# One kernel for memory attention and two MLPs: the first half's instructions keep the order in which the program issues them

## The chip, the core and the metric

The kernel runs on one core of one Trainium2 chip. The metric is the device time of one execution in microseconds (us). Three executions of the kernel before gave 904.52, 904.96 and 908.23 us; their median is 904.96 us.

## What is computed

Three layers run one after the other on B = 4 batches of S = 576 positions (2304 tokens in all). Inputs and weights of the attention are float32; the weights of the two MLPs arrive as float64 and are read as pairs of 32-bit words.

```
a    = softmax over s of phi                      # [b, h, s, 32]
k_m  = einsum('bhsm,bhsd->bhmd', a, k);  v_m the same with v
attn = softmax(q @ k_m^T / 8) @ v_m               # 8 heads of 64
x    = attn as [2304, 512];  xn = x / rms(x) * rms_g
y    = (silu(xn @ w_gate) * (xn @ w_val)) @ w_out     # 512 -> 1536 -> 512
h    = y @ w_in;   g = h if h >= 1, 0 if h <= -1, else (h + 1)^2 / 4
out  = g @ w_out2                                  # 512 -> 2048 -> 512
```

## The kernel before, in words

The program has two halves. **P1** does the attention, the gated MLP and all the turning of weights; its result x2 goes to DRAM as a high and a low part (`x2h_d`, `x2l_d`). **P2** is the second MLP: a plain loop over 5 blocks of tokens and 16 pieces of the inner dimension (`p2_in`, L1034, and `p2_out`, L1059). Every large product is three matmuls (high x high, high x low, low x high).

P1 is a set of Python generators ("streams") that an `Agenda` runs against a model of time. A stream yields what its next step needs: an engine and a duration ("V", 0.69 is 0.69 us of VectorE; P is TensorE, A ScalarE, G GpSimd, D a transfer), a buffer to take or give back, or a flag that another stream sets. The Agenda picks again and again the step that can start first by its model, the lower priority number first among equals, and lets that stream emit its instructions. So the program's order is a schedule worked out by a model of time. The streams are:

- `loads` (L350 on): phi, k, v and q of batch 0, 1, 2, 3 by SP's queue, with model times 1.8 us (phi), 3.6 us each (k, v), 3.4 us (q), 0.45 us each (the four parts of the rest of q), and 1.415 us more until a load has arrived (`DMA_LAG`). The order is phi, k and v, q of batch 0, the same of batch 1, then phi, k and v of batch 2, the rest of q, q of batch 2, and phi, k and v, q of batch 3.
- `soft(b)`: the maximum, difference (L446) and exponential (L453) of phi, then the sums on GpSimd (L460 to L463). Its model times up to the exponential are V 2.12, P 0.25, V 0.29, V 0.42, P 0.3, V 1.35. `memory(b)`: k_m and v_m (kvps, L495) in PSUM banks 7 and 4, then their scaling and `vT`, `vbd`, `kmT`.
- `pair(n)`, nine of them: scores (L621), softmax (L631 to L655), transposes, product with v_m (xp, L684), the norm (L675, L696 to L700), and the split into `Ah`, `Al` (L717, L719).
- `chunk(fc)`, 12 of them, and `convert`: a 512 KB transfer into one of 4 `raw` buffers (L245, model time 1.46), then the float64 words become float32: exponent part on VectorE or ScalarE (L261 or L259), low word on GpSimd or ScalarE (L266 or L264), merged on VectorE (L270), and the sign set on VectorE (L274); the last two have a model time of 0.69 each. A chunk of w_gate and w_val fills a `w` buffer (3 of them, and 2 more in the place of `w2s`) and is stored to DRAM (L325) for the later batches. `wo1_unit` does the same for w_out and `w2_piece` for the second MLP, with a split into high and low (L283, L285).
- `vw`: v_m times a chunk (L763, in PSUM banks 6 and 7), after which the `w` buffer is free; its split is L781, L783. `gv`: the gate and value products (L812, six matmuls each for a half of the positions), and `gate`: L837, L840, L843, L845. `out1`: L870, three matmuls for each of 12 chunks (one step of 0.395, after a flag of that chunk's gate), and x2's split and store (L884 to L894).
- `heat`: small matmuls (L474) that only keep TensorE busy in the beginning.

What the program emits is then ordered anew: a scheduler of the language, with a timing simulation of its own, sorts the instructions of every engine by when it thinks that they are ready. `keep_in_program_order` pins an instruction behind the one that was emitted before it on the same engine; the kernel before uses it for the loads of phi, k, v, q, for the first 24 raw transfers and for the heat matmuls, and for nothing else. Three lines carry the model of what follows what:

```python
HOP = {"P": 0.14, "V": 0.16, "A": 0.16, "G": 0.16, "D": 1.2, "PP": 0.0, "VV": 0.12, "AA": 0.12, "GG": 0.1}
self.free = {"D": 1.7}
starts = [max(at + HOP.get(x[5] + e, HOP[e]), self.free.get(e, 0.0)) for e in kind[: len(times)]]
```

`x[5]` is the engine of the stream's last step: a step on the same engine costs the smaller hop ("PP": 0.0). Passing a flag empties `x[5]`, so that the next step pays the hop of an engine that has to be told by another.

Of the kernel before, what the change touches and what calls it, by code (L numbers as in the profile page):

```python
# [25 lines left out]
ORDER = [0, 1, 2, 3, 8, 4, 5, 6, 7]  # L26

BANKS = {"g": (0, 1), "v": (2, 3), "o": (4, 5), "p": (0, 1, 2, 3), "w": (6, 7), "q": (2, 3), "s": (1,), "x": (2, 3), "a": (0,), "t": (5,), "k": (7,), "m": (4,), "l": (4,)}

KEEP = 24  # L30

HEAT = (6, ("A", (0, 0)), 2.09, 0.34)

# [11 lines left out]
class Agenda:  # L45
# [59 lines left out]
    def run(self, stop=None):  # L105
        while self.live and not (stop and stop in self.flags):
            best = None
            for x in self.live:
                s = self._start(x)
                if s is not None:  # L110
                    key = (max(s[0], self.now), x[0], x[1])
                    if best is None or key < best[0]:
                        best = key, x, s[1]
            assert best is not None, [(x[0], x[3]) for x in self.live]
            (at, _, _), x, z = best
            self.live.remove(x)
            self.now = at
            kind, arg = x[3]
            value = None
            done = at  # L120
            if kind == "take":
                self.room[arg] -= 1
            elif kind == "give":
                self.room[arg] += 1
            elif kind == "rest":
                done += arg
            elif kind == "flag":
                x[5] = ""
            elif kind == "heat":
                tick = int(at / TICK)  # L130
                value = self.ticks.get(tick, 0.0) < HEAT[2]
                if value:
                    slow = 1.0 if self.ticks.get(tick - 1, 0.0) > WARM else 2.0
                    self.ticks[tick] = self.ticks.get(tick, 0.0) + arg
                    done = self.free["P"] = at + arg * slow
            else:
                value = kind[z]
                t = arg[z] if isinstance(arg, tuple) else arg
                if value == "P":
                    tick = int(at / TICK)  # L140
                    slow = 1.0 if self.ticks.get(tick - 1, 0.0) > WARM else 2.0
                    self.ticks[tick] = self.ticks.get(tick, 0.0) + t * DUTY.get(kind, 1.0)
                    t *= slow
                done = self.free[value] = at + t
                x[5] = value
            self.done = done
            x[4] = x[4] + 0.5 if kind == "Dq" else done
            self._go(x, value)


def tile_attn_moe(tc, q, k, v, phi, w_gate, w_val, w_out1, rms_g, w_in2, w_out2, out):
# [10 lines left out]
    nc = tc.nc  # L162
    B, H, S, D = q.shape
    M = phi.shape[3]
# [72 lines left out]
    def convert(src, pieces, dst, split, done):  # L237

        yield "take", "raw"
        yield "D", 1.46  # L240
        n = nconv[0]
        nconv[0] += 1
        raw = wv.tile([P, CU, 2], U32, tag="raw", name=f"raw{n}", bufs=BUFS["raw"])
        rs = raw.rearrange("p n t -> p (n t)")
        i = nc.sync.dma_start(out=rs.rearrange("p (c f) -> p c f", c=pieces) if pieces > 1 else rs, in_=src)  # L245
        if n < KEEP:
            tc.keep_in_program_order(i)
        yield "rest", DMA_LAG
        if split:
            yield "take", "x"  # L250
            x = wv.tile([P, CU], F32, tag="x", name=f"cx{n}", bufs=BUFS["x"])
            dst = x
        hv, low = raw[:, :, 1].bitcast(F32), raw[:, :, 0]
        if len(dst.shape) > 2:
            hv, low = (t.rearrange("p (c f) -> p c f", c=dst.shape[1]) for t in (hv, low))
        du = dst.bitcast(U32)
        eng = yield "VAhi", (0.45, 0.68)
        if eng == "A":
            nc.scalar.activation(out=dst, in_=hv, func=AF.Copy, scale=SHRINK)  # L259
        else:  # L260
            nc.vector.tensor_scalar(out=dst, in0=hv, scalar1=SHRINK, scalar2=None, op0=ALU.mult)  # L261
        eng = yield "GAlow", (0.73, 0.68)
        if eng == "A":
            nc.scalar.activation(out=low, in_=low, func=AF.Copy, scale=LOW_SCALE, bias=LOW_BIAS)  # L264
        else:
            nc.gpsimd.tensor_scalar(  # L266
                out=low, in0=low, scalar1=LOW_SCALE, scalar2=LOW_BIAS, op0=ALU.mult, op1=ALU.add
            )
        yield "V", 0.69
        nc.vector.scalar_tensor_tensor(  # L270
            out=du, in0=du, scalar=3, in1=low, op0=ALU.logical_shift_left, op1=ALU.bitwise_or
        )
        yield "V", 0.69
        nc.vector.scalar_tensor_tensor(  # L274
            out=du, in0=hv.bitcast(U32), scalar=0x80000000, in1=du, op0=ALU.bitwise_and, op1=ALU.bitwise_or
        )
        yield "give", "raw"
        if split:
            hi, lo = split
            if len(hi.shape) > 2:  # L280
                x = x.rearrange("p (c f) -> p c f", c=hi.shape[1])
            yield "A", 0.63
            nc.scalar.activation(out=hi, in_=x, func=AF.Copy)  # L283
            eng = yield "VGlo", (0.69, 1.35)
            (nc.vector if eng == "V" else nc.gpsimd).tensor_tensor(  # L285
                out=lo, in0=x, in1=hi.bitcast(F32), op=ALU.subtract
            )
            yield "give", "x"
        done()
# [60 lines left out]
    def loads():  # L350

        seq = []
        for b in range(B):
            seq += [("phi", b), ("kv", b)]
        for i, pr in zip(Q_AT, q_loads, strict=True):
            seq.insert(i, ("q", pr))
        for s in seq:
            yield "take", "qr" if s[0] == "q" and s[1][0] == B else s[0]
            if s[0] == "phi":
                b = s[1]  # L360
                yield "Dq", 1.8
                t = phi_t[b] = ld.tile([P, 4, J, M], F32, tag="phi", name=f"phi{b}", bufs=BUFS["phi"])
                tc.keep_in_program_order(
                    nc.sync.dma_start(out=t.rearrange("p c j m -> p c (j m)"), in_=by_half(phi[b], J * M))
                )
            elif s[0] == "kv":
                b = s[1]
                t = kv_t[b] = ld.tile([P, 2, 4, J, D], F32, tag="kv", name=f"kv{b}", bufs=BUFS["kv"])
                for i, src in ((0, k), (1, v)):
                    yield "Dq", 3.6  # L370
                    tc.keep_in_program_order(
                        nc.sync.dma_start(
                            out=t[:, i].rearrange("p c j d -> p c (j d)"), in_=by_half(src[b], J * D)
                        )
                    )
            else:
                b = s[1][0]
                yield "Dq", 3.4 if b < B else 0.45 * len(per_batch(s[1]))
                if b == B:
                    t = q_t[s[1]] = ld.tile([P, H, LJ, D], F32, tag="qr", name=f"qr{s[1][1]}", bufs=BUFS["qr"])  # L380
                    for bb, rows in per_batch(s[1]):
                        tc.keep_in_program_order(
                            nc.sync.dma_start(
                                out=t[rows],
                                in_=q[bb, :, SM:S, :].rearrange("h (p j) d -> p h j d", j=LJ),
                            )
                        )
                else:
                    t = q_t[s[1]] = ld.tile([P, H, QJ, D], F32, tag="q", name=f"q{b}", bufs=BUFS["q"])
                    tc.keep_in_program_order(  # L390
                        nc.sync.dma_start(
                            out=t.rearrange("p h j d -> p h (j d)"),
                            in_=q[b, :, 0:SM, :].rearrange("h (p j) d -> p h (j d)", j=QJ),
                        )
                    )
            add(0, arrived(s))
        for name in ("phi", "kv", "q", "qr"):
            for _ in range(BUFS[name]):
                yield "take", name
        mark("inputs")  # L400
# [66 lines left out]
    def heat():  # L467
# [3 lines left out]
        while HEAT[1] not in agenda.flags:  # L471
            go = yield "heat", 0.1067
            if go:
                i = nc.tensor.matmul(  # L474
                    out=t[:, 0:256], lhsT=zeros[:, 0:P], rhs=zeros, start=True, stop=True,
                    skip_group_check=True,
                )
                tc.keep_in_program_order(i)
        yield "give", ("bank", HEAT[0])

    s1_t = {}
# [452 lines left out]
            mark("w2 done")  # L934


    add(0, loads())
    for b in range(B):
        add(P_SOFT + 2 * b, soft(b))
# [76 lines left out]
    for i in range(N2U, N2U + N2R):  # L1016
        load_w2(2 * i + 1, w2c)
    agenda.run()
    left.close()


# [114 lines left out]
```

## Time and profile before

| | us |
|---|---|
| median of three executions | 904.96 |
| the profiled execution, its own time | 907.72 |
| its span | 905.9 |
| TensorE busy in the span | 853.7 |
| VectorE busy | 468.6 |
| ScalarE busy | 333.6 |
| GpSimd busy | 106.4 |
| first matmul of P2 (L1034) | 493.6 |

The span is what the profiler saw of the program, and 1.8 us of the execution lie around it. Matmuls are pipelined, so TensorE's busy time covers overlapping work. The interesting part is P1, from 0 to 493.6 us; after it TensorE runs the two products of P2 one after the other to the end.

### The profile page before, as it was taken

To read this page: it belongs to the slowest core of one execution; us is meant where nothing else is said; L and a number is where in the kernel's file an instruction comes from. 1 tells how busy PE (TensorE), PEld (TensorE's weight loads), DVE (VectorE), ACT (ScalarE), POOL (GpSimd) and SP (SyncE) were. 2 spreads that over 40 slices of the span, in tenths; PEclk is the share of its full clock that TensorE was granted. 3 is DMA by queue.
4 is the path that set the end of the run, shared out by engine and by line. 5 is a ranking of instruction groups with operands and counts; after the bars stand their busy time and mean duration, and the time that the engine had idled before them with its cause. 6 is when DMAs were issued, how large, how long until landed. Compare 5 with 4: busy or idle time off the path is not lost.

```text
span 905.9 us, 15047 instructions
## 1 busy us (share of the span) xinstructions
PE 853.7 (94%) x6058; PEld 732.8 (81%) x6058; DVE 468.6 (52%) x836; ACT 333.6 (37%) x656; POOL 106.4 (12%) x160
## 2 busy tenths in 40 slices
PE   7767889979999999999999999999999999999992
PEld 6655678859988998899999888888888888888892
DVE  3566857987898685405521433433343333333441
ACT  2335556645577355304421222222222222222330
POOL 3135314510000020000020500000000000000000
PEclk9886979969999999999999999999999999999997
DMA  9987233769999998222383980000040003000100
GB/s 321 329 281 244 95 117 111 263 228 330 346 338 342 358 317 291 103 79 94 120 253 111 387 260 1 25 22 1 1 140 0 1 1 93 0 1 1 47 1 24
DMA packets 72142, 137.56 MB, mean 152 GB/s; under 512 B 8840, under 2 KB 37512, under 8 KB 72072
## 3 DMA queue, kind: packets, MB, share of 16 engines
q1 hardware_dynamic: 61576, 108.28, 34.8%
q0 software_dynamic: 10496, 28.32, 10.0%
q8 instruction: 47, 0.77, 0.3%
q14 instruction: 23, 0.19, 0.1%
HBM read 99.35 MB, written 37.22 MB: 151 GB/s over the span
## 4 chain that ended last, share of the span: by engine, by line
PE 83%; DMA 7%; DVE 5%; ACT 2%; issue 1%; POOL 1%; SPq 0%; DVEq 0%; ACTq 0%
PE acc L1059 22%; PE hp L1034 22%; PE ops L870 16%; PE gps L812 7%; PE vps L812 7%; PE vwps L763 3%; DMA raw<-in_moe_w_gate_dram 2%; PE xp L684 2%; DMA phi<-in_phi_dram 1%; DMA raw<-in_moe_w_out_dram 1%; DMA raw<-in_moe_w_val_dram 1%; DVE w L270 1%; DVE w L274 1%; PE heat L474 1%; DMA raw<-in_moe_w_in_dram 1%
## 5 line engine op out<-in xcount | busy, mean ns | idle before, releaser
L1034 PE MATMUL hp<-xh,w 128*128 128x512 f32 (+1 forms) x640 | 193.1, 368 | 0.0
L1059 PE MATMUL acc<-w,gh 128*128 128x512 f32 x576 | 178.4, 391 | 0.0
L1034 PEld LDWEIGHTS hp<-xh,w 128*128 128x128 f32 x640 | 117.0, 188 | 21.5
L1040 DVE SCALAR_TENSOR_TENSOR y<-y 128x512 f32<-128x512 f32 (+1 forms) x80 | 51.1, 639 | 152.0 <-ACT y L1039 152.0
L1059 PEld LDWEIGHTS acc<-w,gh 128*128 128x128 f32 x576 | 107.0, 188 | 22.4
L1034 PE MATMUL hp<-xl,w 128*128 128x512 f32 (+1 forms) x320 | 118.3, 370 | 0.0
L870 PE MATMUL ops<-ah,wo1h 128*128 128x288 f32 x384 | 113.2, 297 | 2.1 <-ACT ah L843 2.1
L870 PE MATMUL ops<-al,wo1h 128*128 128x288 f32 x384 | 113.6, 297 | 1.3 <-DVE al L845 0.7
L870 PE MATMUL ops<-ah,wo1l 128*128 128x288 f32 x384 | 112.9, 295 | 0.1
L1059 PE MATMUL acc<-w,gl 128*128 128x512 f32 x288 | 112.6, 392 | 0.0
L1039 ACT ACTIVATE y<-hp,consts 128x512 f32<-128x512 f32 (+1 forms) x80 | 51.6, 645 | 151.7 <-PE hp L1034 151.7
L1044 ACT ACTIVATE gh<-y 128x512 fp32r<-128x512 f32 (+1 forms) x80 | 47.1, 589 | 137.5 <-PE acc L1059 118.5
L1045 DVE TENSOR_TENSOR gl<-y,gh 128x512 fp32r<-128x512 f32 (+1 forms) x80 | 51.1, 639 | 79.9 <-ACT gh L1044 79.9
L870 PEld LDWEIGHTS ops<-ah,wo1h 128*128 128x128 f32 x384 | 71.9, 188 | 4.2 <-ACT ah L843 2.6
L870 PEld LDWEIGHTS ops<-al,wo1h 128*128 128x128 f32 x384 | 72.3, 188 | 3.2 <-POOL al L845 1.5
L870 PEld LDWEIGHTS ops<-ah,wo1l 128*128 128x128 f32 x384 | 72.2, 188 | 0.3 <-DVE wo1l L285 0.3
L1034 PEld LDWEIGHTS hp<-xl,w 128*128 128x128 f32 x320 | 60.2, 188 | 10.8
L1059 PEld LDWEIGHTS acc<-w,gl 128*128 128x128 f32 x288 | 54.0, 188 | 12.3
L812 PE MATMUL gps<-Ah,vwh 128*128 128x288 f32 x192 | 60.7, 316 | 2.0 <-ACT vwh L781 2.0
L843 ACT ACTIVATE ah<-th 128x288 fp32r<-128x288 f32 x96 | 42.0, 442 | 47.7 <-DVE th L840 47.4
L812 PE MATMUL vps<-Ah,vwh 128*128 128x288 f32 x192 | 58.4, 304 | 0.0
L840 DVE TENSOR_TENSOR th<-th,vps 128x288 f32<-128x288 f32 x96 | 42.9, 449 | 29.4 <-PE vps L812 29.4
(116 smaller groups left out, 1366.0 us busy)
## 6 DMA issues: line engine op xcount, KB each, us to landing
w<-wf_d SPq DMA_DIRECT2D x36, 512.0 KB, 4.4
w<-w_d POOLq DMA_DIRECT2D x36, 512.0 KB, 8.1
w_d<-w2s SPq DMA_DIRECT2D x32, 512.0 KB, 6.2
raw<-in_moe_w_out_dram SPq DMA_DIRECT2D x28, 512.0 KB, 5.5
raw<-in_moe_w_in_dram SPq DMA_DIRECT2D x16, 512.0 KB, 5.6
raw<-in_moe_w_gate_dram SPq DMA_DIRECT2D x12, 512.0 KB, 6.7
raw<-in_moe_w_val_dram SPq DMA_DIRECT2D x12, 512.0 KB, 6.1
wf_d<-w SPq DMA_DIRECT2D x12, 512.0 KB, 4.4
```

Of the source, the lines that this page charges most:

```text
L684: nc.tensor.matmul(out=xp[rows, 256 * g : 256 * g + 256], lhsT=aT[:, i, g, rows], rhs=vbd_t[bb][:, g].rearrange("p h d -> p (h d)"), start ...
L763: nc.tensor.matmul(out=vps[g][0][32 * c : 32 * c + 32, 2 * P * x : 2 * P * x + 2 * P], lhsT=vT[b][hs, c, :], rhs=t[hs, c].rearrange("p i f ...
L812: nc.tensor.matmul(out=p[:, 0:HB], lhsT=wt[:, g, i, :], rhs=at[b][:, g, c], start=(g == 0 and x == 0), stop=(g == 1 and x == 2),)
L840: nc.vector.tensor_tensor(out=th, in0=th, in1=ps[1][0], op=ALU.mult)
L843: nc.scalar.activation(out=ah, in_=th, func=AF.Copy)
L870: nc.tensor.matmul(out=p[:, 0:HB], lhsT=wt[:, fc, d], rhs=at[:, c], start=(fc == 0 and x == 0), stop=(fc == NF1 - 1 and x == 2),)
L1034: nc.tensor.matmul(out=hp, lhsT=wt[:, kc, :], rhs=xt[:, kc, 0:n], start=(kc == 0 and x == 0), stop=(kc == KC - 1 and x == 2),)
L1039: nc.scalar.activation(out=y, in_=hp, func=AF.Relu, scale=0.5, bias=half)
L1040: nc.vector.scalar_tensor_tensor(out=y, in0=y, scalar=1.0, in1=y, op0=ALU.min, op1=ALU.mult)
L1044: nc.scalar.activation(out=gh, in_=y, func=AF.Copy)
L1045: nc.vector.tensor_tensor(out=gl, in0=y, in1=gh.bitcast(F32), op=ALU.subtract)
L1059: nc.tensor.matmul(out=acc, lhsT=gt[:, cs], rhs=wt, start=(fc == 0 and x == 0), stop=(fc == NF2 - 1 and x == 2),)
```

## The change

The whole of P1 is emitted inside a context in which each engine, and each queue of transfers, issues its instructions in the order in which the program emitted them; P2 stays as it was. The pins are dropped, as that context holds every instruction. In the Agenda, a flag that had already been set when the stream came to it leaves `x[5]` as it is. The sign of the weights stays on VectorE (L274), and no instruction is added or removed by the text of the change; the Agenda may put a step on another engine or at another place, since its model of time has changed.

```diff
-KEEP = 24
...
             elif kind == "flag":
-                x[5] = ""
+                if at > x[4]:
+                    x[5] = ""
...
-        i = nc.sync.dma_start(out=rs.rearrange("p (c f) -> p c f", c=pieces) if pieces > 1 else rs, in_=src)
-        if n < KEEP:
-            tc.keep_in_program_order(i)
+        nc.sync.dma_start(out=rs.rearrange("p (c f) -> p c f", c=pieces) if pieces > 1 else rs, in_=src)
...
-                tc.keep_in_program_order(
-                    nc.sync.dma_start(out=t.rearrange("p c j m -> p c (j m)"), in_=by_half(phi[b], J * M))
-                )
+                nc.sync.dma_start(out=t.rearrange("p c j m -> p c (j m)"), in_=by_half(phi[b], J * M))
...
-                i = nc.tensor.matmul(
+                nc.tensor.matmul(
                     out=t[:, 0:256], lhsT=zeros[:, 0:P], rhs=zeros, start=True, stop=True,
                     skip_group_check=True,
                 )
-                tc.keep_in_program_order(i)
...
+    order = ExitStack()
+    order.enter_context(tc.manual_schedule())
     add(0, loads())
...
     agenda.run()
+    order.close()
     left.close()
```

## Rows read from the trace of the kernel before

**Rows 1.** Page, part 2: TensorE's busy tenths and granted clock in 40 slices
```profile
PE   7767889979999999999999999999999999999992
...
PEclk9886979969999999999999999999999999999997
```

**Rows 2.** Stages: stretch, its length; busy PE, PEld, DVE, ACT, POOL; clock; DMA
```profile
48.30:54.10 5.80, 1.71 (x16) 1.46 (x15) 0.00 (x0) 0.00 (x0) 0.00 (x0) 1.00 1.09 349
54.10:82.00 27.90, 18.12 (x216) 13.62 (x217) 25.89 (x47) 15.62 (x29) 12.33 (x14) 0.63 0.86 284
82.00:98.50 16.50, 16.10 (x239) 11.76 (x239) 8.57 (x20) 8.77 (x19) 8.87 (x13) 0.91 0.17 52
98.50:140.00 41.50, 35.92 (x321) 28.68 (x316) 26.00 (x51) 23.58 (x54) 10.60 (x16) 0.88 0.35 115
140.00:200.00 60.00, 54.00 (x422) 43.82 (x421) 53.60 (x88) 36.51 (x78) 23.43 (x26) 0.89 0.62 206
200.00:340.00 140.00, 139.42 (x1195) 127.23 (x1193) 116.02 (x224) 81.53 (x171) 12.14 (x16) 1.00 0.96 338
340.00:493.50 153.50, 153.50 (x1330) 145.91 (x1323) 55.59 (x116) 50.37 (x116) 8.75 (x15) 1.00 0.45 150
```

**Rows 3.** VectorE and ScalarE in order of time, 46 to 55 us
```profile
46.93 1.35 DVE L446 TENSOR_TENSOR phi<-phi,mps 128x1152 f32<-128x1152 f32 x1 [0.41 <-PE mps L440]
54.12 0.43 DVE L261 TENSOR_SCALAR w<-raw 128x512 f32<-128x512 f32 x1 [5.83 <-DMA raw<-in_moe_w_gate_dram]
54.12 0.67 ACT L264 ACTIVATE raw<-raw 128x512 uint32<-128x512 uint32 x1 [5.84 <-DMA raw<-in_moe_w_gate_dram]
54.69 1.15 ACT L453 ACTIVATE phi<-phi 128x1152 f32<-128x1152 f32 x1
```

**Rows 4.** Memory chain of batch 3 and chunk 5, in order of time
```profile
80.34 1.35 DVE L446 TENSOR_TENSOR phi<-phi,mps 128x1152 f32<-128x1152 f32 x1
84.06 1.16 ACT L453 ACTIVATE phi<-phi 128x1152 f32<-128x1152 f32 x1
97.87 1.05 PE L763 MATMUL vwps<-w,vT 64*32 64x256 f32 x12
98.56 0.43 DVE L261 TENSOR_SCALAR w<-raw 128x512 f32<-128x512 f32 x1 [1.79 <-PE vwps L763]
```

**Rows 5.** Waits of SP's queue: total us, times, longest
```profile
SPq L245 <- DVE w L274: 47.1, 8, 29.0
SPq L325 <- DVE w L274: 39.4, 10, 20.9
```

**Rows 6.** Chain of waits, in order of time: start, length, what
```profile
124.24 0.19 PE gps L812
...
214.47 27.42 PE ops L870 x207
493.58 10.24 PE hp L1034 x45
```

**Rows 7.** Waits of TensorE and its weight loads, 200 to 493.5 us
```profile
PE ops L870 <- ACT ah L843: 0.6, 1, 0.6
PEld gps L812 <- ACT ah L843: 3.3, 8, 0.4
```

**Rows 8.** Groups of instructions: busy us, mean ns, idle before
```profile
L274 DVE SCALAR_TENSOR_TENSOR w<-raw,w 128x512 uint32<-128x512 uint32 x24 | 20.5, 856 | 0.1
L274 DVE SCALAR_TENSOR_TENSOR cx<-raw,cx 128x512 uint32<-128x512 uint32 x44 | 32.9, 752 | 0.3
L837 ACT ACTIVATE th<-gps 128x288 f32<-128x288 f32 x96 | 38.7, 407 | 16.4 <-PE gps L812 13.3 <-POOL al L845 1.2 <-PE vwps L763 0.8
L840 DVE TENSOR_TENSOR th<-th,vps 128x288 f32<-128x288 f32 x96 | 42.9, 449 | 29.4 <-PE vps L812 29.4
L843 ACT ACTIVATE ah<-th 128x288 fp32r<-128x288 f32 x96 | 42.0, 442 | 47.7 <-DVE th L840 47.4
L845 DVE TENSOR_TENSOR al<-th,ah 128x288 fp32r<-128x288 f32 x81 | 38.5, 479 | 21.2 <-ACT ah L843 20.9
```

More of the change, by code (lines that the diff above doesn't have):

```diff
@@ L370, in loads @@
                     yield "Dq", 3.6
[L371 to L374, printed above, removed]
+                    nc.sync.dma_start(
+                        out=t[:, i].rearrange("p c j d -> p c (j d)"), in_=by_half(src[b], J * D)
                     )
@@ L381, in loads @@
                     for bb, rows in per_batch(s[1]):
[L382 to L386, printed above, removed]
+                        nc.sync.dma_start(
+                            out=t[rows],
+                            in_=q[bb, :, SM:S, :].rearrange("h (p j) d -> p h j d", j=LJ),
                         )
@@ L389, in loads @@
                     t = q_t[s[1]] = ld.tile([P, H, QJ, D], F32, tag="q", name=f"q{b}", bufs=BUFS["q"])
[L390 to L394, printed above, removed]
+                    nc.sync.dma_start(
+                        out=t.rearrange("p h j d -> p h (j d)"),
+                        in_=q[b, :, 0:SM, :].rearrange("h (p j) d -> p h (j d)", j=QJ),
                     )
```

## The prediction

> **What bounds the kernel now.** I read the page's slices first [rows 1]: TensorE is at nine tenths or more from the tenth slice on, and its clock is full there, so anything that can be won lies in the first 200 us or so. Next the chain of waits: P2's first product starts at 493.58, and inside the full stretch 207 matmuls of out1 take 27.42 us, 0.1325 each, with nothing between them [rows 6]. P1 from 200 us on is 293.5 us in which TensorE is never short of work [rows 2], and P2 with what follows is about 412 us more (905.9 - 493.6). Neither can shrink by a change of order alone. So the end is set by how early TensorE becomes full.
>
> The stages before that show what keeps TensorE from being full [rows 2]. None of the engines is full there: TensorE has holes and a granted clock of 0.63 between 54 and 82 us (the slower of its two levels, 1.2 instead of 2.4 GHz, for most of that stretch), and the DMA share falls from 1.09 to 0.17 and 0.35. VectorE has the most work that all others wait for, and yet it idles 5.8 us of 48.3 to 54.1, 2.0 of the next stretch (27.90 - 25.89), 7.9 of the next (16.50 - 8.57), 15.5 of the next (41.50 - 26.00) and 6.4 of the last (60.00 - 53.60): **37.6 us of 151.7**, with 114.1 us of work. The holes come from order. From 48.3 VectorE and ScalarE both stand before the first weights' transfer for 5.83 us, while the exponential of phi of batch 2 (L453), whose input was finished at 46.93 + 1.35 = 48.28, is queued behind that conversion [rows 3]. Then VectorE converts weights while batch 3's memory chain waits: its difference comes at 80.34 and its exponential at 84.06. PSUM bank 7, which that chain's kvps takes (BANKS: k is 7, w is 6 and 7), is needed by the second half of every vw product; so vw comes at 97.87, and chunk 5's conversion, which needs a buffer that vw frees, waits for it until 98.56 [rows 4]. Meanwhile SP's queue stands: its longest waits for L274 are 20.9 and 29.0 us [rows 5], the time with hardly any transfer.
>
> **The change part by part.** *The order of P1.* By the Agenda's own numbers, batch 2's phi has landed at 1.7 + 3 x 1.8 + 4 x 3.6 + 2 x 3.4 + 1.4 = 29.7 us, and its exponential starts some 5.6 us later (4.7 of steps, the rest hops). The first weights land at 1.7 + 51.4 + 1.46 + 1.4 = 56.0, after all 51.4 us of attention loads; the trace has them at 54.1 [rows 3], so the model of transfers is good here. In the program's order that exponential, and batch 3's (phi at 43.9, start near 49.5), therefore stand ahead of the first conversion. When an engine then waits for the weights, what could run has been issued already: 5.8 us won. Late next is only the weights' transfer itself. Batch 3's memory chain then finishes beside the first conversions, instead of having its exponential at 84.06 [rows 4], bank 7 comes free for vw, and the block on chunk 5 goes. The nine pairs' tails (each a string of short steps over four engines) lie beside conversions instead of after them.
>
> How much of the 37.6 us comes back? At most all of it. At least nothing, if new holes take their place. I take the share that VectorE reaches with the same mix of conversions and gates between 140 and 200 us, 53.60 of 60.00, or 0.893 [rows 2], because that is the nearest stage in which work is plentiful: 114.1 / 0.893 = 127.7 us instead of 151.7, **24 us won**. That TensorE can follow: it has 54 us of busy time in the last 60 and much less before, some of it at half clock.
>
> *What is moved past what.* On SP the first 24 raw transfers and the attention loads were pinned already, so their order stays; later reloads of w, stores of x2 and raw transfers go to the Agenda's places. The DMA share of 0.96 from 200 to 340 us [rows 2] would be full either way, and of it only w's reloads are needed by TensorE before P2. On GpSimd the 13 preloads of the second MLP (L970) stay behind the last steps of P1 that they wait for; they have until 493 us, and VectorE, which converts for them, is busy only 55.59 of 153.5 us from 340 on. Cost nothing; if w2 were late by more than that slack, TensorE would wait at P2's start. Dropping the pins and closing the context before P2 cost nothing: P1 is held by the context, and P2's cover is TensorE's own full queue.
>
> *The flag rule.* No instruction changes. Each of out1's 384 steps passes a flag, and in the old model then pays 0.14 us on top of 0.395; the trace shows none of it (3 x 0.1325 = 0.397 [rows 6]). So the plan had 384 x 0.14 = 54 us that do not exist, and now it has not. It moves the places of steps, and alone gains nothing where TensorE is full. I take 0; the lower end is the second rival's.
>
> *New waits.* Nothing can now overtake a step that is late. From 200 us on TensorE waits 0.6 us in all, and its weight loads eight times 0.4 us for ah [rows 7]. I take eight more such waits, 3 us; between nothing and the second rival's price that is nearest to these rows.
> The row for what one late step costs is the 5.83 us [rows 3]. The Trainium skill, in "PSUM — Partial Sum Buffer", section "Engine vs sequencer instructions", says that the queues of ScalarE, VectorE and GpSimd are strictly first in, first out, and that matmuls also complete in program order. The trace agrees in that row. By that rule every late operand under the program's order stops its whole engine, and one wait of this size left in place would give 890 instead of 884.
>
> Sum: 907.72 - 24 + 3 = 886.7 for an execution like the profiled one, which is 2.76 above the median of 904.96; for the median **884 us**.
>
> **The rivals.** *The gain is given back before 340 us.* From 200 to 340 VectorE is busy 116.02 of 140 us and the DMA share is 0.96 [rows 2]: if the weights of the second MLP, early in that queue, hold up reloads of w, TensorE starts to wait where it does not now. Against it: it waits 0.6 us there now [rows 7]. All but 3 of the 24 us lost would give 902.
>
> *Slower: gates late under a fixed order, between 200 and 340 us.* out1's step for a half chunk follows that half's gate: 0.407 + 0.449 + 0.442 + 0.479 = 1.78 us [rows 8], while the two products of the next half give TensorE 12 x 0.1325 = 1.59 us. The Agenda prices each sign merge at 0.69 us; the trace has 0.752 and 0.856 [rows 8]. VectorE so falls behind the plan by 44 x 0.06 + 24 x 0.17 = 6.7 us for L274 alone, and TensorE, in the planned order, meets its operand late. If that costs 0.2 for the difference and one merge of 0.75 for each of some 34 halves that lie in these 140 us (24 halves a batch in about 100 us), it is 32 us; with only half of the front's gain that gives 905 + 32 - 12 = 925. It decides from 24 / 34 = 0.7 us per half on. For it: VectorE is at 0.83 in that stretch. Against it: the plan leaves whole chunks between the gate and its use when out1 lags gv by several chunks, and the drift is spread over 300 us.
>
> *The order hardly changes,* since the scheduler works from the same streams: 905. Against it speak rows 3, in which the program's order and the issued one differ by the planner's own arrival times.
>
> **How the numbers follow.** About 0.5% (4.5 us) is what a measurement of this kernel can tell from no change: faster is below 900.4, slower above 909.5. I give the forecast's case 0.72 (from all 37.6 us, 867, to a quarter of it less the new waits, 898), the gain given back 0.11 (902), no change of order 0.03 (905), the gates 0.14 (910 to 925). So faster 0.72, same 0.14, slower 0.14. The range 866 to 907 leaves out the slower rival and a little at the low end.
>
> **What would show it.** Right: no joint wait of VectorE and ScalarE for the first gate weights with L453 behind it; batch 3's L453 before 65 us; the first gps (L812) near 105 instead of 124 [rows 6]; no SP wait of 20 us on L274; VectorE at 0.85 or more from 48 us to the point where TensorE is full; P2's first product near 472. The prediction is wrong if that product starts at 490 or later, or if TensorE's waits between 200 us and P2 add up to more than 10 us, and its forecast of size if the early stages win but VectorE's share stays near 0.75.

## The result and the profile after

The median of four executions is **884.28 us** (883.12 to 887.02), against 906.55 (904.52 to 908.23) of four of the kernel before: a ratio of 0.976, with a 95% interval of 0.9725 to 0.9794. The profiled execution took 884.17 us, its span is 882.4 us, 23.5 less than before. The prediction said 884.0, with a range of 866 to 907. The total is right; that its two parts are not what the prediction said is the subject of what follows. Lines have moved: L274 is now L271, L453 is L442, L763 is L751, L812 is L800, L837 to L845 are L825 to L833, L870 is L858 and L1034 is L1026.

The chain of waits of the kernel after (start, length, what) answers to [rows 6]:

```profile
187.75 30.80 PE ops L858 x231
...
471.15 10.22 PE hp L1026 x45
```

P2's first product starts 22.4 us earlier (493.58 before). Nearly the whole gain is made by then, so P1 is where to look. The stages of the kernel after, with the columns of [rows 2], and a part of the fifth:

```profile
48.30:54.10 5.80, 5.66 (x44) 5.04 (x44) 4.89 (x11) 3.48 (x9) 3.12 (x5) 1.00 1.09 351
54.10:82.00 27.90, 21.93 (x355) 17.47 (x353) 25.40 (x47) 18.77 (x40) 13.12 (x18) 0.94 0.49 151
82.00:98.50 16.50, 10.29 (x65) 7.44 (x66) 15.54 (x27) 8.96 (x18) 4.87 (x7) 0.69 0.91 305
98.50:140.00 41.50, 31.89 (x266) 26.51 (x266) 29.81 (x58) 25.75 (x58) 11.78 (x15) 0.85 0.51 163
140.00:200.00 60.00, 48.43 (x422) 43.96 (x423) 52.22 (x88) 35.83 (x74) 16.29 (x17) 0.91 0.68 235
...
140.00:176.00 36.00, 24.51 (x196) 21.44 (x196) 35.61 (x57) 23.89 (x48) 14.64 (x15) 0.84 0.80 273
...
200.00:340.00 140.00, 140.00 (x1286) 132.99 (x1285) 95.98 (x189) 67.59 (x151) 9.67 (x13) 1.00 0.76 259
```

The first stage is what was forecast: VectorE and ScalarE work 4.89 and 3.48 us where both stood still [rows 2, 3]. Batch 3's exponential comes at 59.30 instead of 84.06 [rows 4], as VectorE's and ScalarE's instructions in order of time show, and the first gate product comes at 101.7 instead of 124.24 [rows 6]:

```profile
57.13 1.35 DVE L435 TENSOR_TENSOR phi<-phi,mps 128x1152 f32<-128x1152 f32 x1
...
59.30 1.16 ACT L442 ACTIVATE phi<-phi 128x1152 f32<-128x1152 f32 x1
```

The tile gps of the kernel after up to 200 us (duration min/median/max in ns, first and last start):

```profile
L800 PE MATMUL gps<-Ah,vwh x48: 288/295/484, 101.7 to 185.0; 128*128 128x288 f32 x48
```

SP's longest waits for the weights' sign (total, times, longest) are shorter than in [rows 5]; the totals are little less:

```profile
SPq L244 <- DVE w L271: 43.4, 9, 18.1
...
SPq L322 <- DVE w L271: 34.2, 11, 9.5
```

**What was not forecast** stands in the part from 140 to 176 us. VectorE is full there (35.61 of 36.00), and TensorE is busy for only 24.51, at a granted clock of 0.84. TensorE's waits that end between 140 and 200 us are a single line (the longest, 6.7 us, began at 134.8):

```profile
PE vps L800 <- DVE th L828: 16.7, 5, 6.7
```

The time line shows why. The gate's product (L828), which frees the PSUM bank of the next vps, stands behind merges (L267), signs (L271) and splits (L282) of weights, and none of these may be overtaken now. One of the five waits, with VectorE in order of time and ScalarE's and TensorE's line at its two ends:

```profile
157.88 0.41 ACT L825 ACTIVATE th<-gps 128x288 f32<-128x288 f32 x1
158.06 1.15 DVE L271 SCALAR_TENSOR_TENSOR cx<-raw,cx 128x512 uint32<-128x512 uint32 x1
159.13 0.68 DVE L267 SCALAR_TENSOR_TENSOR cx<-cx,raw 128x512 uint32<-128x512 uint32 x1
159.73 0.68 DVE L267 SCALAR_TENSOR_TENSOR w<-w,raw 128x512 uint32<-128x512 uint32 x1
160.33 0.68 DVE L282 TENSOR_TENSOR wo1l<-cx,wo1h 128x512 fp32r<-128x512 f32 x1
...
162.74 0.68 DVE L271 SCALAR_TENSOR_TENSOR w<-raw,w 128x512 uint32<-128x512 uint32 x1
163.34 0.80 DVE L828 TENSOR_TENSOR th<-th,vps 128x288 f32<-128x288 f32 x2
163.84 0.61 PE L800 MATMUL vps<-Ah,vwh 128*128 128x288 f32 x1 [4.37 <-DVE th L828]
```

ScalarE's part of both gates is done by 158.29 and TensorE's last vps before the wait was issued at 156.80, yet VectorE does eight conversion steps from 158.06 on before it comes to the two gates at 163.34; TensorE waits 4.37 us for them. In the longest wait VectorE even stands still in front of a merge whose data has not come, with the gate (140.98) next in its order:

```profile
140.37 0.69 DVE L267 SCALAR_TENSOR_TENSOR w<-w,raw 128x512 uint32<-128x512 uint32 x1 [1.16 <-ACT raw L261]
```

During these two waits the granted clock falls to the lower level (0.50 from 137.6 to 144.4 us, 0.51 from 161.4 to 168.3), and the matmuls behind them start 0.24 us apart instead of 0.1325.

The kernel before had its TensorE full in that time and its hole later, as its own windows (columns of [rows 2]) show:

```profile
140.00:160.00 20.00, 20.00 (x169) 16.95 (x168) 18.77 (x34) 14.40 (x32) 8.11 (x10) 1.00 0.43 134
160.00:180.00 20.00, 19.16 (x159) 17.13 (x158) 18.75 (x30) 13.19 (x29) 10.54 (x11) 1.00 0.83 288
180.00:190.00 10.00, 4.85 (x33) 2.94 (x32) 8.09 (x14) 4.67 (x10) 2.58 (x4) 0.71 0.76 255
```

So how far ahead is the new kernel once TensorE is full? That can be counted. Every record of gps, vps and ops costs 0.1325 us [rows 6], and from 200 us to P2 the kernel before has 444 + 444 + 1092 = 1980 of them, the new one 432 + 432 + 1035 = 1899. The front is worth 81 x 0.1325 = **10.7 us** of products done earlier. The other half of the 22.4 us comes from 200 us on, where TensorE is busy all the time in the kernel after and all but 0.6 us of it in the kernel before.

### The profile page after: what moved, and what is told of

Same layout as the page of the kernel before. It is cut to its first block, busy times and chain, and to the rows that moved or that the text cites. A ratio compares the mean times of both kernels' runs of the same rounds, so it can differ in the third digit from the quotient of the medians.

```text
span 882.4 us, 15006 instructions
## 1 busy us (share of the span) xinstructions
PE 827.1 (94%) x6058; PEld 723.4 (82%) x6058; DVE 469.7 (53%) x842; ACT 328.7 (37%) x652; POOL 103.4 (12%) x158
## 3 DMA queue, kind: packets, MB, share of 16 engines
q0 software_dynamic: 10496, 28.32, 10.3%
## 4 chain that ended last, share of the span: by engine, by line
PE 85%; DVE 6%; DMA 3%; issue 2%; ACT 2%; SPq 0%; ACTq 0%; DVEq 0%
PE acc L1051 22%; PE hp L1026 22%; PE ops L858 17%; PE vps L800 8%; PE gps L800 8%; PE vwps L751 2%; PE xp L672 2%; DVE w L267 1%; DMA raw<-in_moe_w_val_dram 1%; DVE w L271 1%; DMA kv<-in_v_dram 1%; PE kvps L483 1%; DMA raw<-in_moe_w_out_dram 1%; PE sc L609 1%; PE qps L591 1%
## 5 line engine op out<-in xcount | busy, mean ns | idle before, releaser
L1026 PE MATMUL hp<-xh,w 128*128 128x512 f32 (+1 forms) x640 | 193.2, 369 | 0.0
L1026 PEld LDWEIGHTS hp<-xh,w 128*128 128x128 f32 x640 | 117.0, 188 | 21.4
L1051 PEld LDWEIGHTS acc<-w,gh 128*128 128x128 f32 x576 | 107.0, 188 | 22.4
L1026 PE MATMUL hp<-xl,w 128*128 128x512 f32 (+1 forms) x320 | 118.3, 370 | 0.0
L858 PE MATMUL ops<-ah,wo1h 128*128 128x288 f32 x384 | 113.5, 295 | 0.0
L858 PE MATMUL ops<-ah,wo1l 128*128 128x288 f32 x384 | 113.2, 295 | 0.0
L858 PE MATMUL ops<-al,wo1h 128*128 128x288 f32 x384 | 113.1, 295 | 0.0
L800 PE MATMUL vps<-Ah,vwh 128*128 128x288 f32 x192 | 59.4, 309 | 16.7 <-DVE th L828 16.7
L858 PEld LDWEIGHTS ops<-ah,wo1h 128*128 128x128 f32 x384 | 72.1, 188 | 1.2 <-issue 1.2
L858 PEld LDWEIGHTS ops<-al,wo1h 128*128 128x128 f32 x384 | 72.1, 188 | 0.0
L858 PEld LDWEIGHTS ops<-ah,wo1l 128*128 128x128 f32 x384 | 72.0, 188 | 0.0
L1026 PEld LDWEIGHTS hp<-xl,w 128*128 128x128 f32 x320 | 60.3, 188 | 10.7
L800 PE MATMUL gps<-Ah,vwh 128*128 128x288 f32 x192 | 58.1, 302 | 0.1
L800 PE MATMUL gps<-Al,vwh 128*128 128x288 f32 x192 | 57.3, 298 | 0.0
```

The source lines that it names most:

```text
L800: nc.tensor.matmul(out=p[:, 0:HB], lhsT=wt[:, g, i, :], rhs=at[b][:, g, c], start=(g == 0 and x == 0), stop=(g == 1 and x == 2),)
L858: nc.tensor.matmul(out=p[:, 0:HB], lhsT=wt[:, fc, d], rhs=at[:, c], start=(fc == 0 and x == 0), stop=(fc == NF1 - 1 and x == 2),)
L1026: nc.tensor.matmul(out=hp, lhsT=wt[:, kc, :], rhs=xt[:, kc, 0:n], start=(kc == 0 and x == 0), stop=(kc == KC - 1 and x == 2),)
L1051: nc.tensor.matmul(out=acc, lhsT=gt[:, cs], rhs=wt, start=(fc == 0 and x == 0), stop=(fc == NF2 - 1 and x == 2),)
```

## Where the other half comes from: TensorE's visits to small matmuls

vw (L751) uses a 64*32 part of the array for each of its matmuls; gps, vps and ops use all 128*128. Each time TensorE goes from the large ones to the small ones and back I call a visit. TensorE in order of time, the kernel before (start, length, engine, line, operation, tiles, count):

```profile
255.27 0.29 PE L812 MATMUL vps<-Ah,vwl 128*128 128x288 f32 x1
255.49 0.62 PE L763 MATMUL vwps<-w,vT 64*32 64x256 f32 x2
256.04 0.40 PE L812 MATMUL gps<-Ah,vwh 128*128 128x288 f32 x1
256.27 0.29 PE L812 MATMUL gps<-Al,vwh 128*128 128x288 f32 x1
```

and the kernel after:

```profile
225.01 0.29 PE L858 MATMUL ops<-ah,wo1l 128*128 128x288 f32 x1
225.24 1.09 PE L751 MATMUL vwps<-w,vT 64*32 64x256 f32 x32
226.26 0.40 PE L800 MATMUL gps<-Ah,vwh 128*128 128x288 f32 x1
226.50 0.29 PE L800 MATMUL gps<-Al,vwh 128*128 128x288 f32 x1
```

The price of a visit is read from the last large matmul before it to the second one after it (the first is longer, 0.40 us, and the next starts 0.23 or 0.24 behind it), less two ordinary steps of 0.1325. Before: 256.27 - 255.27 - 0.265 = **0.735 us for 2 records**. After: 226.50 - 225.01 - 0.265 = **1.225 us for all 32** of a product. A small piece costs far more than its share of a whole product. Read so over every visit from 200 us to P2, the kernel before makes 30 visits (2 to 12 records at 0.74 to 0.78 us, 18 to 32 records at 1.18 to 1.22, one at 1.32), 30.4 us in all; the kernel after makes 16 whole ones, 19.6 us. The scheduler had cut the products of vw and put the pieces between others, and the program's order keeps each product whole. **10.8 us** come back, in a stretch that looks full in both. Some 0.9 of them belong to the front, since the kernel before has 536 records of vw left at 200 us and the kernel after 512; the cuts are the other 9.9.

The 0.735 us are not all a price of changing the shape. In the code the 16 matmuls of a product (two records each) use eight different 64*32 parts of the array, each of them twice. In the trace records on different parts start 0.007 us apart, and the next record on the same part 0.22 to 0.24 us later: the parts work side by side. So a visit that uses each part at most once costs 0.74 to 0.79 us, with 2 records (kernel before) or 16 (e7), and in the kernel before each visit that uses some part twice, counted in the program's order, costs 1.18 or more. A piece therefore pays twice: for going there and back (0.325 us for one visit more, by e7 below), and for work that would have lain beside other work (the rest of the 0.735; an estimate, by difference).

The Trainium skill says in "TensorEngine Tiling (Array Packing)", section "Tiling Modes", that a change of tiling mode drains TensorE; the drain itself cannot be seen in these traces, but a price for going there and back can, 0.325 us by e7. The busy share hides what the visits cost; the weight loads do not. The window from 200 us to P2 of the kernel before, with the columns of [rows 2] (the second pair is the weight loads'):

```profile
200.00:493.40 293.40, 292.82 (x2516) 273.04 (x2515) 171.61 (x339) 131.90 (x286) 20.89 (x31) 1.00 0.69 240
```

and of the kernel after:

```profile
200.00:471.00 271.00, 271.00 (x2412) 259.81 (x2411) 158.30 (x315) 115.58 (x259) 21.12 (x33) 1.00 0.73 245
```

That is 293.40 - 273.04 = 20.4 us without a weight load against 271.00 - 259.81 = 11.2. The page "Perfetto Trace Analysis" of the Trainium skill, section "Identifying the Most-Contended Engine", warns that matmul busy time is no good measure of how close TensorE is to its limit, and names the weight loads' share; here the trace bears that out (TensorE busy 292.82 of 293.40 us, its weight loads 273.04).

With the step of 0.1325 us and each kernel's own visits, read from its trace, the time from 200 us to P2 can be accounted for in every kernel of this study whose TensorE is full by 200 us, as 200 + large records x 0.1325 + visits:

| kernel | median us | large records left at 200 | visits, us in all | worked out | P2 starts at |
|---|---|---|---|---|---|
| before | 906.55 | 1980 | 30, 30.4 | 492.8 | 493.4 |
| after | 884.28 | 1899 | 16, 19.6 | 471.2 | 471.0 |
| e1 flag only | 913.21 | 1970 | 46, 41.1 | 502.1 | 501.9 |
| e2 old flag | 894.70 | 1895 | 16, 19.7 | 470.8 | 480.4 |
| e3 front only | 896.82 | 1831 | 47, 40.7 | 483.3 | 483.1 |
| e4 back only | 903.67 | 2032 | 17, 20.8 | 490.0 | 490.5 |
| e7 products in two | 884.31 | 1880 | 32, 25.3 | 474.4 | 474.0 |
| e8 al on GpSimd | 880.08 | 1860 | 16, 19.7 | 466.2 | 466.7 |
| e9 slower merges | 881.75 | 1887 | 16, 19.5 | 469.5 | 469.4 |
| e10 both of these | 880.13 | 1848 | 16, 19.5 | 464.4 | 464.3 |
| e11 products in four | 925.72 | 1953 | 64, 50.9 | 509.7 | 509.9 |
| e12 open middle | 875.38 | 1836 | 16, 19.5 | 462.8 | 463.3 |

All but e2 agree within 0.6 us, so nothing else of size lies in that stretch; what is left in e2 are waits (below). The counts are of records, and the columns from the fourth on are of one profiled execution, which can lie some us off the median.

## The experiments

The kernel before ran on the same chips in 907.27 us (e1 to e4), 906.19 (e5 to e8), 906.53 (e9 to e11) and 906.31 (e12). Ratios are to it.

**e1: the flag rule alone**, in the kernel before.

```diff
             elif kind == "flag":
-                x[5] = ""
+                if at > x[4]:
+                    x[5] = ""
```

> The kernel before with the flag rule alone; the scheduler sorts as before. Theory (the order of the front makes the gain): the plan changes but the scheduler sorts it anew, so 900 to 911 us and P2's first product near 493. Rival (the corrected model of time makes the gain): 893 us or less.

Measured: 913.21 us (909.35 to 915.11), ratio 1.0057 (1.0027 to 1.0087). It is a little slower, above the range of its theory and far from its rival's. The front is hardly changed (1970 records left instead of 1980), but the scheduler, given this program, makes 46 visits instead of 30: 10.7 us more.

**e2: the change without the flag rule.**

```diff
             elif kind == "flag":
-                if at > x[4]:
-                    x[5] = ""
+                x[5] = ""
```

> The changed kernel with the old flag rule: P1 in the program's order, planned with the hop that out1 does not pay. Theory: the front is planned nearly alike, so 879 to 891 us, VectorE at 0.85 or more of 48 to 140 us. Rival (the corrected model makes the gain): 897 us or more.

Measured: 894.70 us (893.62 to 896.05), ratio 0.9875 (0.9851 to 0.99). A miss: under a fixed order the rule is worth about 10 us. The work left at 200 us and the visits are those of the kernel after; TensorE's waits from 200 us on are not, as it had none there:

```profile
PE gps L799 <- ACT th L824: 5.0, 3, 2.3
PE ops L857 <- DVE xl L873: 1.8, 2, 1.6
```

They name 6.8 of the 9.6 us that the sum lacks. The time line shows the rest: the steps at TensorE's waits are 8.0 us over the ordinary one and the first step behind each some 0.1 us over it, and after the wait of 2.3 us the granted clock is 0.50 for 3.4 us, in which 14 steps take 0.24 us each instead of 0.1325 (1.5 us). Together they make up the 9.6 to within half a microsecond:

```profile
314.00:317.40 3.40, 3.40 (x17) 3.40 (x16) 2.83 (x7) 1.84 (x5) 0.67 (x1) 0.50 0.88 305
```

That the plan, which prices out1 too long, puts other steps in the wrong place against it, and that nothing corrects this under a kept order, would explain these waits; it was not tested.

**e3: the order held up to the end of the attention only, and e4: from there on only** (e3's diff is against the kernel after; e4's is against the kernel before with the flag rule, with its pins on 16 transfers instead of 24).

```diff
     agenda.run("attention")
+    order.close()
...
     agenda.run()
-    order.close()
```

> The changed kernel, with the program's order held only until the attention is emitted, and the scheduler free after that. Theory: at least two thirds of the gain, 882 to 891 us, with batch 3's exponential of phi before 65 us. Rival (the order of gv, out1 and the later conversions makes the gain): 898 us or more.

```diff
-KEEP = 24
+KEEP = 16
...
     agenda.run("attention")
+    order = ExitStack()
+    order.enter_context(tc.manual_schedule())
...
     agenda.run()
+    order.close()
```

> The opposite: scheduler (and pins) until the attention is emitted, the program's order from there on, flag rule as changed. Theory: at most a third of the gain, 898 to 909 us, with the wait of VectorE and ScalarE for the first weights still there near 48 to 54 us. Rival (the later order makes the gain): 890 us or less.

Measured: e3 896.82 us (896.61 to 898.93), ratio 0.9903 (0.9878 to 0.9928), between its two cases; e4 903.67 (901.96 to 905.68), ratio 0.996 (0.9941 to 0.9979), as expected. Neither half of the order gives the whole gain. e3 has the better front, (1980 - 1831) x 0.1325 = 19.7 us ahead of the kernel before at 200 us, and then gives 10.3 us back by 47 visits instead of 30. (The expectation of e12 below says 21.6; it would be 21.5 if the 46 records of vw that e3 has done more were counted too, at 1.22 us for 32.) e4 has few visits and a late front. TensorE's waits for the gates' product (th, L828 of the kernel after) between 140 and 200 us are 15.6 us in e4 and 1.6 in e3, so it is the kept order behind the attention that makes those waits.

**e5: VectorE and ScalarE alone keep the program's order, and e6: TensorE alone** (the kernel before with the flag rule; each instruction of the named engines pinned behind the one emitted before it). The diff is e5's; in e6 PINNED is `('PE',)`.

```diff
+PINNED = ('DVE', 'Activation')
...
+                    self.tc.add_manual_dep(
+                        i, self.last[engine],
...
+                        reason="keep_in_program_order",
```

> The kernel before with the flag rule, and in P1 VectorE and ScalarE alone held in the program's order (each instruction pinned behind the one before it); TensorE, GpSimd and the queues as the scheduler sorts them. Theory now (one half of the gain is the front's order on these two engines, the other half a faster pace of the full TensorE, which has fewer changes between 64x32 and 128x128 matmuls when it keeps the program's order): the front's half alone, 895 to 904 us, batch 3's exponential before 65 us, but from the full stretch on still 20 us or more over the sum of its matmuls. Rival (all is in the order of VectorE and ScalarE): 890 us or less.

> The same with TensorE alone held in the program's order. Theory now: changes of tile shape in the full stretch fall from 102 to 38 and its 20 us over the sum of its matmuls nearly vanish, so 890 to 900 us, with the front as slow as before. Rival (the pace has nothing to do with TensorE's own order): 907 us or more.

Measured: e5 933.11 us (931.12 to 933.39), ratio 1.0299 (1.0266 to 1.0333); e6 914.47 (912.20 to 915.15), ratio 1.0088 (1.0058 to 1.0118). Both missed by far, in the same direction: in these two runs an order kept on some engines beside the scheduler's on the others is worse than either order on all. In e5 VectorE's window (columns of [rows 2]) is emptier than ever:

```profile
48.30:82.00 33.70, 22.70 (x385) 19.75 (x385) 15.46 (x32) 12.18 (x28) 13.01 (x19) 0.80 0.27 86
```

It is busy 15.46 of 33.70 us, and batch 3's exponential comes at 77.3. Its longest wait there is for a matmul of batch 2's memory chain, which TensorE could not start since it waited 9.5 us for a sum on GpSimd, an engine whose order was left to the scheduler. GpSimd had that sum queued behind a weight's low word, for whose transfer it stood 11.70 us:

```profile
DVE r L538 <- PE kvps L528: 10.3, 1, 10.3
...
56.12 0.64 POOL L286 TENSOR_SCALAR raw<-raw 128x512 uint32<-128x512 uint32 x1 [11.70 <-DMA raw<-in_moe_w_val_dram]
```

In e6 the longest of TensorE's waits from 140 to 200 us is for a sign on VectorE, whose order was left to the scheduler:

```profile
PE vwps L783 <- DVE w L294: 10.7, 1, 10.7
```

e6 makes 17 visits from 200 us on (20.8 us): TensorE's own order alone removes the cuts.

**e7 and e11: more visits**, in the kernel after. e7 asks for a pause between the two halves of each vw product, e11 cuts each into four with pauses; the same matmuls are issued.

```diff
             for x in range(2):
+                if x:
+                    yield "rest", 1.0
                 yield "Pw", 0.87
```

> The changed kernel with a rest of 1 us in the plan between the two halves of a vw product, so that other matmuls come between them: 72 changes of tile shape after out1's first matmul instead of 38, all else planned alike. Theory now (about 0.28 us for a change): 9 us slower, 890 to 897 us, with no new waits of TensorE. Rival (changes cost nothing, it was the mixing of sums in different banks): 881 to 888 us.

```diff
+                for half in range(2):
+                    if x or half:
+                        yield "rest", 0.9
+                    yield "Pw", 0.435
...
+                        for c in (2 * half, 2 * half + 1):
```

> The changed kernel with each vw product cut into four parts with other matmuls between: 152 changes of tile shape after out1's first matmul instead of 38. Theory (a visit of TensorE to 64x32 tiles costs a fixed time besides its matmuls; 16 more visits cost 5.4 us of TensorE's pace after 200 us when they were doubled): 48 more visits after 200 us cost 14 to 28 us, 895 to 912 us, and TensorE waits for nothing more than before. Rival (visits are free): 881 to 888 us.

Measured: e7 884.31 us (883.26 to 887.86), ratio 0.9766 (0.9733 to 0.98), no different from the kernel after and in the range of the rival, by which changes cost nothing; e11 925.72 (923.12 to 926.96), ratio 1.0212 (1.0167 to 1.0258), dearer than either case. Both expectations went by a fixed price per change of shape or visit; the time lines show that it matters which parts a piece leaves idle. TensorE in e7, half a product in a visit:

```profile
222.53 0.29 PE L860 MATMUL ops<-ah,wo1l 128*128 128x288 f32 x1
222.74 0.66 PE L753 MATMUL vwps<-w,vT 64*32 64x256 f32 x16
223.34 0.40 PE L802 MATMUL gps<-Ah,vwh 128*128 128x288 f32 x1
223.57 0.29 PE L802 MATMUL gps<-Al,vwh 128*128 128x288 f32 x1
```

and in e11, a quarter (four of the eight parts):

```profile
235.08 0.30 PE L803 MATMUL vps<-Ah,vwl 128*128 128x288 f32 x1
235.30 0.64 PE L754 MATMUL vwps<-w,vT 64*32 64x256 f32 x8
235.87 0.40 PE L803 MATMUL gps<-Ah,vwh 128*128 128x288 f32 x1
236.11 0.29 PE L803 MATMUL gps<-Al,vwh 128*128 128x288 f32 x1
```

By the same reading 16 records cost 223.57 - 222.53 - 0.265 = 0.775 us and 8 cost 0.765. Cutting a product in two, where each half uses every part once, so costs 2 x 0.775 - 1.225 = 0.325 us; in four, where each half's work is done in two turns, 4 x 0.765 - 1.225 = 1.835. For the 16 products after 200 us that is 5.2 and 29.4 us; the visits in all grew by 5.7 and 31.3 (table). In e7 the front came out 2.5 us better (1880 records left), and its profiled execution is the slowest of its four, so the total alone would have refuted the mechanism that its trace confirms. In e11 the front is 54 x 0.1325 = 7.2 us behind that of the kernel after as well.

**e8, e9, e10: the waits for th.** e8 lowers the planner's bias against GpSimd for al (L833) and for w_out's low part, so that GpSimd takes 86 of the 96 al instead of 9; e9 lets the planner count each merge at 0.76 us instead of 0.69; e10 does both.

```diff
-BIAS = {"VAhi": 0.0, "GAlow": 0, "VGlo": 3.746, "VGsum": -99, "GVe": -2.397, "VGal": 0.2, "VGvbd": -0.2}
+BIAS = {"VAhi": 0.0, "GAlow": 0, "VGlo": 0.0, "VGsum": -99, "GVe": -2.397, "VGal": -0.4, "VGvbd": -0.2}
```

> The changed kernel with the plan's preference for GpSimd raised for the low parts (al of the gates: 86 instead of 9 on GpSimd; of wo1: 1 instead of 0). Theory now: from 140 to 176 us VectorE is full and TensorE waits 16.7 us for its th steps, so taking about 0.46 us for a low part off VectorE makes TensorE full earlier: 872 to 881 us. Rival (GpSimd's al of about 1 us is later for out1 than VectorE's, and TensorE waits for it instead): 884 us or more.

```diff
-        yield "V", 0.69
+        yield "V", 0.76
...
-        yield "V", 0.69
+        yield "V", 0.76
```

> The changed kernel with the plan's price of the two merges on VectorE raised from 0.69 to 0.76 us, near what the trace has (0.715 to 0.805). Theory (VectorE falls behind a plan that prices its conversions too low, and TensorE, in the planned order, waits 16.7 us for th from 140 to 176 us): the waits fall below 10 us and the time to 874 to 881 us. Rival (VectorE is simply full there; no plan helps): 882 us or more, waits as before.

> The price of the merges and the preference of GpSimd for the low parts together. Theory: the two add up in part, 870 to 879 us. Rival (they remove the same waits): as the better of the two alone, 878 to 882 us.

Measured: e8 880.08 us (878.38 to 880.32), ratio 0.9709 (0.9681 to 0.9737); e9 881.75 (880.91 to 882.59), ratio 0.9723 (0.9686 to 0.976); e10 880.13 (877.68 to 882.74), ratio 0.9706 (0.9664 to 0.9747). All intervals overlap that of the kernel after, so a gain of some 4 us is likely for e8 and no more than that; e8 and e10 lie at the slow end of what was expected (e10 in its rival's range, so the two do not add). e9 is not told apart from the kernel after by its time; its waits for th from 140 to 200 us are 9.9 us, just below the expected 10, and e10's are 11.5. With less work on VectorE, TensorE's waits shrink in e8 but stay:

```profile
PE vps L800 <- DVE th L828: 9.3, 6, 3.0
PE gps L800 <- ACT th L825: 1.2, 1, 1.2
...
```

**e12: the order held up to the end of the attention and again from batch 0's last gate on; open between.** The table says that e3's front and the kernel after's visits should add up.

```diff
     agenda.run("attention")
+    order.close()
...
     agenda.run(("a", NF1 - 1, 1))
+    order.enter_context(tc.manual_schedule())
```

> The program's order is held up to the end of the attention and again from the last gate of batch 0 on; between the two the scheduler may move instructions, as in the version whose order is held up to the attention alone. That version reached 200 us with 21.6 us of the products ahead of the kernel before, and then lost 21 us after it to 47 visits of TensorE to the small matmuls of vw (40.7 us; the changed kernel has 16 visits, 19.6 us). Theory: both gains are kept; the front is that version's and the visits are 17 or so. Its 896.8 less 20 gives 877: 872 to 882, P2's first product near 462, TensorE's visits to vw after 200 us about 20 us in all. Rival A: the planned order after the opening does not fit the front that the scheduler made, and TensorE waits for gates as it did where only the back was held (15.6 us): 885 to 895. Rival B: the scheduler's front and the planned one are the same where VectorE is full, so that nothing is won over the changed kernel: 883 to 886.

Measured: **875.38 us** (874.69 to 876.51), ratio 0.9656 (0.9635 to 0.9676), as the theory said, and faster than both kernels: its interval lies below that of the kernel after. Its stage from 140 to 176 us, with the columns of [rows 2]:

```profile
140.00:176.00 36.00, 31.45 (x280) 25.59 (x261) 34.86 (x57) 24.14 (x53) 13.18 (x15) 1.00 0.79 272
```

VectorE's gates in that stretch (line, engine, operation, tiles, count, then busy us and mean ns of one, and idle time before), in e12:

```profile
L828 DVE TENSOR_TENSOR th<-th,vps 128x288 f32<-128x288 f32 x14 | 6.0, 443 | 0.8 <-ACT th L825 0.8
```

and in the kernel after:

```profile
L828 DVE TENSOR_TENSOR th<-th,vps 128x288 f32<-128x288 f32 x11 | 4.7, 443 | 0.0
```

VectorE is just as full (34.86 of 36.00 us), but in the same time it does 14 gates instead of 11 and 22 merges and signs (L267, L271) instead of 28. TensorE gets 31.45 us instead of 24.51, at a clock of 1.00 instead of 0.84, and from 140 us to P2 its waits for th are 2.5 us (4.6 for everything) instead of 16.7. This speaks for a loss by which of VectorE's steps came first, and not for want of VectorE's time. That VectorE's order alone does it is not shown: e12 leaves the other engines to the scheduler as well, and of the 60 large records that it is ahead of the kernel after at 176 us, it has 16 at 140 us already. The front is now (1980 - 1836) x 0.1325 = 19.1 us ahead of the kernel before, against 10.7 in the kernel after, and the 16 visits are kept.

## Why the prediction was right, and where it was not

**The holes of 48 to 140 us: right, by its mechanism.** The joint wait is gone, batch 3's exponential comes before 65 us, the first gps near 105 (101.7), no SP wait on the sign reaches 20 us, and VectorE's share from 48.3 us to 176, where TensorE becomes full, is (4.89 + 25.40 + 15.54 + 29.81 + 35.61) / 127.7 = 0.871, near the 0.893 that was taken. e4, with the scheduler's order in the front, loses it.

**The front, 24 us less 3: mis-sized, it was worth 10.7.** TensorE does become full about 24 us earlier, at 176 instead of 200, and VectorE has done nearly the same work by then (111.25 us of it from 48.3 us on, against 114.06). But the step from there to the end took VectorE's work as the measure of TensorE's, and the kernel after has started only 246 large matmuls by 176 us, the kernel before 326 by 200: 80 x 0.1325 = 10.6 us of the 24 are missing. VectorE did conversions first and gates late (18 gates by 176 us, against 21 by 200), and the kernel before had filled TensorE from 140 to 180 us, ahead of its last hole. The term at fault is the *3 us for new waits*. The waits are 16.7 us, with steps at half speed behind them. Their mechanism was written down, as the slower rival (gates behind merges on a full VectorE), and its condition, VectorE full, was looked for between 200 and 340 us; it was met from 140 to 176. In e3 and e12, with that stretch left to the scheduler, the front is worth 19.7 and 19.1 us, not far from 24 less 3.

**"Neither can shrink by a change of order alone": wrong.** This sentence on the stretch from 200 us on rested on a busy share of 1.00 and on *one* pure run of out1 [rows 6]. Some 10 us of that stretch were the scheduler's cut products. The numbers were in the rows read: weight loads busy 127.23 of 140.00 us from 200 to 340 [rows 2], now 132.99.

**The flag rule at nothing: wrong by about 10 us with the order kept** (e2). Alone it is 6 us slower (e1), and there by the visits. In these two runs its worth depends on who uses the plan.

**The fixed order after 200 us and P2: right.** TensorE waits for nothing from 200 us to P2 in the kernel after; the gain is not given back there, and P2 keeps its length (412.3 us from its first product to the end of the span before, 411.2 after).

So that 884.0 met 884.28 is luck: the front was counted 10 us too high and the full stretch some 10 us too low. What stays open: why e2's plan makes TensorE wait after 200 us, why the scheduler cuts the products of vw more often with the flag rule, and whether VectorE's order alone makes the waits from 140 to 176 us.

## What to carry to other kernels

An engine that is busy all the time can still be made faster by order: count its work by kind, price each kind by a pure run, and see whether the sum gives the length of the stretch; here what was over were visits to another tile shape, which took 0.74 us with two records in them and 0.78 with sixteen. Here the fixed order paid in the front and on TensorE's visits, and cost where VectorE was full and the gates stood behind conversions, so hold an order stretch by stretch and look at each stretch's waits. And when a total agrees with a forecast, check its terms one by one: here two errors of 10 us cancelled.

## What the runs showed of the hardware

- 2, 8 and 16 records of the small matmuls take nearly the same time between large ones (0.735, 0.765 and 0.775 us a visit) as long as no 64*32 part of the array is used twice; 32, with each part used twice, take 1.225. Records on different parts start 0.007 us apart in the trace. The busy share of TensorE is 1.00 through all of it.
- One visit more, with the same work side by side, cost 0.325 us (e7).
- The first large matmul after a visit lasts 0.40 us instead of 0.29, and the next starts 0.23 or 0.24 us behind it instead of 0.13. The same is seen after a plain wait (at 156.03 us of the kernel after, behind a wait of 2.34 us).
- The granted clock was 0.84 in the stretch in which TensorE waited for gates (24.51 of 36.00 us busy) and 1.00 in the same stretch of e12 (31.45 busy). Large matmuls started 0.24 us apart at the lower level and 0.1325 at the higher.
